# Preparing f64 weights in small VectorE steps, transposing k on TensorE, and fixed places for staged weights, in attention followed by two MLPs

## The chip, the cores and the metric

The kernel runs on one core of one Trainium2 chip. The metric is the device time of one execution in microseconds (us), lower is better. The engines are named as the profile names them: PE (TensorE, matmuls), PEld (its weight loads), DVE (VectorE), ACT (ScalarE), POOL (GpSimd) and SP (SyncE, which here only issues DMAs). Each engine works through its own instructions in order; a DMA issue is an instruction of the engine that issues it.

## The reference

Linear attention over 8 batches and 8 heads, then two MLPs on the 4608 tokens, one after the other. All arithmetic is f32; the weights arrive as f64.

```python
q_s = softmax(q, axis=-1)             # over head_dim 64, q is (8, 8, 576, 64)
k_s = softmax(k, axis=2)              # over the 576 positions
kv = np.einsum('bhsd,bhse->bhde', k_s, v)
x = np.einsum('bhsd,bhde->bhse', q_s, kv)
x = x.transpose(0, 2, 1, 3).reshape(4608, 512)
h = x @ w_in1;  x = (h * sigmoid(h)) @ w_out1              # (512, 2048), (2048, 512)
h = x @ w_in2;  out = (h * clip(h + 3, 0, 6) / 6) @ w_out2
```

## The kernel before

**Cycles.** The work on PE is a list of 144 cycles, g = 0 to 143. A cycle takes one block of 512 tokens and one pair p (0 to 7) of 128-column tiles of w_in with the matching rows of w_out; nine token blocks make one MLP, so cycles 0 to 71 are the first MLP and 72 to 143 the second. Cycles 0 to 7 (`first_cycle`, the first token block) use plain f32 matmuls. From cycle 8 on, `cycle` uses Strassen's scheme on split operands: seven `product`s of 128x256 matmuls into the PSUM banks A, B and C, each of three matmuls (high and low parts), and eight pieces `G` of the output product of the cycle before, into y. Bank A's left half is copied to B by ACT (L653), DVE adds s = B + s5 (L664), A + s (L669) and B + s5 (L674); then `bend` applies the activation (ACT L515 or L517, DVE L519) and splits the result into gs. PE can start its next product into B only when DVE has read B at L664. Bank D serves the attention. `side(k)`, k = 0 to 7, is called between the pieces of a cycle; there the attention and the weight preparation are woven in, and the order of these calls is the order of the instructions on each engine.

**Attention.** A unit u is a batch and two heads, 32 units. The four units of batch 0 run ahead of the cycles, those of batch 1 within cycles 0 to 7, the others later; `events` maps a tick (8 g + k) to the calls. In batch 1 the exponent of k in its natural layout is made by sending the row maximum through DRAM (`at_sendnm`, L304: nmd<-nm; `at_shift`, L310: nb<-nmd, both issued on ACT), a subtraction on POOL (`at_sub`, L315) and an exp on ACT (`at_exp`, L319).

**Weights.** A pair is staged as 1 MB of f64 words (st<-w_dram, `feed`, L90, on SP) and turned into f32 by `converting`: Abs on ACT into a tile "size" (L99), then four DVE instructions (L101, L102, L107, L112). For w_in, `operands_w` makes four sums s (L155) and splits both into the 1.8 MB operand "ring" (or r), high part on ACT, low part on DVE; `keep_w` stores it to DRAM (wd, on SP), and `load_w` brings it back two cycles ahead of its use (ring<-wd). For w_out, `split_out` makes woh (ACT) and wol (DVE). The first MLP's weights are prepared in cycles 0 to 14; the second's from cycle 56 on. There "size" shares one buffer ("ok") with the sums s. Staging has two buffers in both places. These functions are generators: each `yield` ends a step, and `pump(k)` takes k steps, whatever they cost:

```python
            if late and g > LATE:
                pump({NC - 2: (1, 0, 0, 0, 1, 1, 0, 0), NC - 1: (1, 0, 0, 0, 0, 1, 0, 0)}.get(p, (2, 0, 0, 0, 1, 1, 2, 0))[k])
```

Of the kernel before, what the change touches and what calls it, by code (L numbers as in the profile page):

```python
# [8 lines left out]
F32 = mybir.dt.float32  # L9
# [8 lines left out]
P = 128  # L18
# [17 lines left out]
def attention_two_mlps(ctx: ExitStack, tc: tile.TileContext, kqT, kv5, qn, w1, w2, out):  # L36
# [26 lines left out]
    def bank(name):  # L63
        if "D" in banks:
            return banks["D"]
        return banks["pool"].tile([P, 512], F32, tag="b", name=name)
# [14 lines left out]
    fed = [0]  # L81

    def feed(k=1):
        for m, p, i in stream[:k]:
            if m == 0:
                t = z_p.tile([P, 2 * DM, 2], U32, tag=f"z{fed[0] % 2}", name="st")
            else:
                t = m2_p[0].tile([P, 2 * DM, 2], U32, tag="st", name="st", bufs=2)
            fed[0] += 1
            nc.sync.dma_start(out=t.rearrange("p n w -> p (n w)"), in_=(w1, w2)[m][i, p])  # L90
            staged[m, p, i] = t
        del stream[:k]

    def converting(w, m, p, i):
        t = staged.pop((m, p, i))
        low, high = t[:, :, 0], t[:, :, 1]
        bits = w.bitcast(U32)
        size = (z_p if m == 0 else m2_p[0]).tile([P, 2 * DM], F32, tag="z3" if m == 0 else "ok", name="size")
        nc.scalar.activation(out=size, in_=f32(high), func=AF.Abs)  # L99
        yield  # L100
        nc.vector.tensor_scalar_max(size, size, SMALLEST)  # L101
        nc.vector.tensor_scalar(  # L102
            out=bits, in0=size.bitcast(U32), scalar1=3, scalar2=0x3FFFFFF8,
            op0=ALU.logical_shift_left, op1=ALU.bitwise_and,
        )
        yield
        nc.vector.scalar_tensor_tensor(  # L107
            out=bits, in0=high, scalar=0xC0000000, in1=bits,
            op0=ALU.bitwise_and, op1=ALU.bitwise_or,
        )  # L110
        yield
        nc.vector.scalar_tensor_tensor(  # L112
            out=bits, in0=low, scalar=29, in1=bits,
            op0=ALU.logical_shift_right, op1=ALU.bitwise_or,
        )
        if m == 0:
            feed()

    active = []

    def pump(k):
        while active and k > 0:
            try:
                next(active[0])
            except StopIteration:
                active.pop(0)
            k -= 1
# [7 lines left out]
    def convert_in(p):  # L135
        raw_in[p] = w = w_pool[p].tile([P, 2 * DM], F32, tag=f"a{p}", name="wi")
        yield from converting(w, 0, p, 0)

    def convert_out(p):
        raw_out[p] = w = w_pool[p].tile([P, 2 * DM], F32, tag=f"b{p}", name="wo")  # L140
        yield from converting(w, 0, p, 1)
# [5 lines left out]
    def operands_w(r, w, s):  # L147

        a22, a11, a12, a21 = (w[:, j * 256:(j + 1) * 256] for j in range(4))
        s1, s2, s3, s4 = (s[:, j * 256:(j + 1) * 256] for j in range(4))  # L150
        for o, x, y, op in (
            (s1, a21, a22, ALU.add), (s2, s1, a11, ALU.subtract),
            (s3, a11, a21, ALU.subtract), (s4, a12, s2, ALU.subtract),
        ):
            nc.vector.tensor_tensor(out=o, in0=x, in1=y, op=op)  # L155
        yield
        w3, s4 = (t.rearrange("p (s n) -> p s n", n=256) for t in (w[:, :768], s))
        split(r[:, 0, :3], r[:, 1, :3], w3)
        yield
        split(r[:, 0, 3:], r[:, 1, 3:], s4)  # L160

    def keep_w(m, p, r):
        wd[m, p] = d = dram.tile([P, 14 * 256], F32, tag=f"wd{m}{p}", name="wd")
        nc.sync.dma_start(out=d, in_=f32(r).rearrange("p h s n -> p (h s n)"))

    def prepare_in(p):
        r = ring_tile(NC + p)
        s = z_p.tile([P, 2 * DM], F32, tag="z2", name="s")
        yield from operands_w(r, raw_in.pop(p), s)
        yield  # L170
        yield
        keep_w(0, p, r)

    def split_out(m, p, w):
        h = w_pool[p].tile([P, 2 * DM], F32R, tag=f"a{p}", name="woh")
        q = (p - 1) % 9
        l = w_pool[q].tile([P, 2 * DM], F32R, tag=f"b{q}", name="wol")
        split(h, l, w)
        wo[m, p] = h, l

    def second_in(p):
        w = m2_p[0].tile([P, 2 * DM], F32, tag="w", name="w")
        yield from converting(w, 1, p, 0)
        yield
        s = m2_p[0].tile([P, 2 * DM], F32, tag="ok", name="s")
        r = m2_p[0].tile([P, 2, 7, 2 * P], F32R, tag="r", name="r")
        feed()
        yield from operands_w(r, w, s)
        yield
        keep_w(1, p, r)  # L190

    def second_out(p):
        w = m2_p[0].tile([P, 2 * DM], F32, tag="w", name="w")
        yield from converting(w, 1, p, 1)
        yield
        feed()
        split_out(1, p, w)
# [145 lines left out]
    def at_trk(u):  # L343
        k, e = un[u]["k"], un[u]["e"]
        b0, b1 = bank("tk0"), bank("tk1")
        for j in range(4):
            nc.tensor.transpose(b0[:, j * P:(j + 1) * P], k[:, j * P:(j + 1) * P], ident)
# [528 lines left out]
```

## Time and profile before

| | |
|---|---|
| median of 3 runs (lowest, highest) | 1767.19 us (1765.88, 1771.6) |
| the profiled execution | 1764.48 us, its span 1762.4 us |
| PE busy | 1659.3 us (94%) |
| DVE busy | 1044.0 us (59%) |
| ACT busy | 739.9 us (42%) |
| POOL busy | 185.4 us (11%) |
| DMA | 400.59 MB, mean 227 GB/s |

The span counts from the first to the last instruction; 2.1 us of the execution lie around it. Busy shares are means over the whole span, and its stages differ: the rows further down take them apart by stage, with the first matmul into bank C as the mark of a cycle.

### The profile page before, as it was taken

To read this page: it belongs to the slowest core of one execution; us is meant where nothing else is said; L and a number is where in the kernel's file an instruction comes from. 1 tells how busy PE (TensorE), PEld (TensorE's weight loads), DVE (VectorE), ACT (ScalarE), POOL (GpSimd) and SP (SyncE) were. 2 spreads that over 40 slices of the span, in tenths; PEclk is the share of its full clock that TensorE was granted. 3 is DMA by queue.
4 is the path that set the end of the run, shared out by engine and by line. 5 is a ranking of instruction groups with operands and counts; after the bars stand their busy time and mean duration, and the time that the engine had idled before them with its cause. 6 is when DMAs were issued, how large, how long until landed. Compare 5 with 4: busy or idle time off the path is not lost.

```text
span 1762.4 us, 25043 instructions
## 1 busy us (share of the span) xinstructions
PE 1659.3 (94%) x9796; PEld 1423.1 (81%) x9796; DVE 1044.0 (59%) x1733; ACT 739.9 (42%) x1392; POOL 185.4 (11%) x128
## 2 busy tenths in 40 slices
PE   7788999999999999999998899999999999999994
PEld 4334887888888898897777789999999999999994
DVE  7888677465656657467877764545453535353531
ACT  5434555444544445444444433333343434343431
POOL 2221223222222122200000000000000000000000
PEclk9899999999999999999999999999999999999997
DMA  8789969999999999868886746564546555555540
GB/s 218 226 264 274 269 161 283 252 228 248 235 281 256 229 243 260 241 236 328 308 308 270 290 164 226 186 227 168 215 172 227 185 223 189 194 200 207 207 169 24
DMA packets 72189, 400.59 MB, mean 227 GB/s; under 512 B 20872, under 2 KB 24456, under 8 KB 46472
## 3 DMA queue, kind: packets, MB, share of 16 engines
q1 hardware_dynamic: 70920, 398.72, 71.8%
q8 instruction: 78, 1.28, 0.3%
q10 hardware_dynamic: 1152, 0.26, 0.1%
q14 instruction: 39, 0.32, 0.1%
HBM read 350.49 MB, written 48.47 MB: 226 GB/s over the span
## 4 chain that ended last, share of the span: by engine, by line
PE 67%; DMA 14%; DVE 11%; ACT 4%; issue 2%; SPq 1%; POOL 0%; ACTq 0%; DVEq 0%; POOLq 0%
PE y L73 11%; PE y L74 11%; PE y L75 11%; PE B L73 5%; PE B L75 5%; PE B L74 5%; PE A L73 4%; DMA ring<-wd 4%; PE A L74 4%; PE A L75 4%; DMA q<-qn_dram 3%; DMA nmd<-nm 2%; DMA st<-w_dram 2%; PE C L75 1%; PE C L73 1%
## 5 line engine op out<-in xcount | busy, mean ns | idle before, releaser
L70 DVE TENSOR_TENSOR gs<-g,gs 128x512 fp32r<-128x512 f32 x272 | 195.3, 718 | 151.7 <-ACT gs L69 150.6
L73 PE MATMUL B<-o,ring 128*128 128x256 f32 x816 | 234.7, 288 | 37.3 <-DVE s L664 24.2
L69 ACT CAST gs<-g 128x512 fp32r<-128x512 f32 x272 | 168.6, 620 | 206.5 <-DVE g L519 206.1
L73 PE MATMUL A<-op,ring 128*128 128x256 f32 x816 | 232.7, 285 | 12.6 <-DMA ring<-wd 10.4
L74 PE MATMUL A<-op,ring 128*128 128x256 f32 x816 | 232.1, 284 | 1.2 <-DVE op L70 1.1
L75 PE MATMUL A<-op,ring 128*128 128x256 f32 x816 | 231.7, 284 | 0.0
L75 PE MATMUL B<-o,ring 128*128 128x256 f32 x816 | 230.7, 283 | 0.0
L74 PE MATMUL B<-o,ring 128*128 128x256 f32 x816 | 230.4, 282 | 0.0
L73 PE MATMUL y<-woh,gs 128*128 128x512 f32 x576 | 227.8, 395 | 0.0
L74 PE MATMUL y<-wol,gs 128*128 128x512 f32 x576 | 227.8, 395 | 0.0
L75 PE MATMUL y<-woh,gs 128*128 128x512 f32 x576 | 224.5, 390 | 0.0
L73 PEld LDWEIGHTS B<-o,ring 128*128 128x128 f32 x816 | 154.9, 190 | 72.5 <-DVE s L664 36.7
L73 PE MATMUL y<-gs,woh 128*128 128x512 f32 x512 | 205.4, 401 | 0.0
L74 PE MATMUL y<-gs,woh 128*128 128x512 f32 x512 | 203.1, 397 | 0.0
L75 PE MATMUL y<-gs,wol 128*128 128x512 f32 x512 | 200.9, 392 | 0.0
L73 PEld LDWEIGHTS A<-op,ring 128*128 128x128 f32 x816 | 156.7, 192 | 22.7 <-ACT o L69 4.2
L74 PEld LDWEIGHTS B<-o,ring 128*128 128x128 f32 x816 | 154.8, 190 | 15.1 <-issue 0.5
L74 PEld LDWEIGHTS A<-op,ring 128*128 128x128 f32 x816 | 156.9, 192 | 7.5 <-DVE op L70 2.1
L75 PEld LDWEIGHTS A<-op,ring 128*128 128x128 f32 x816 | 157.0, 192 | 0.0
L75 PEld LDWEIGHTS B<-o,ring 128*128 128x128 f32 x816 | 154.6, 189 | 0.0
L517 ACT ACTIVATE g<-A,half 128x512 f32<-128x512 f32 x72 | 49.6, 688 | 247.8 <-DVE A L669 247.8
L664 DVE TENSOR_TENSOR s<-B,s 128x256 f32<-128x256 f32 x136 | 57.3, 421 | 152.0 <-PE B L75 150.0
(145 smaller groups left out, 2993.3 us busy)
## 6 DMA issues: line engine op xcount, KB each, us to landing
ring<-wd SPq DMA_DIRECT2D x134, 1792.0 KB, 7.9
st<-w_dram SPq DMA_DIRECT2D x32, 1024.0 KB, 9.0
ev<-kv_dram SPq DMA_DIRECT2D x28, 640.0 KB, 9.9
wd<-ring SPq DMA_DIRECT2D x8, 1792.0 KB, 13.8
wd<-r SPq DMA_DIRECT2D x8, 1792.0 KB, 10.5
kq<-kqT_dram SPq DMA_DIRECT2D x24, 576.0 KB, 8.1
q<-qn_dram SPq DMA_DIRECT2D x32, 288.0 KB, 8.8
yd<-y SPq DMA_DIRECT2D x9, 1024.0 KB, 12.2
```

Of the source, the lines that this page charges most:

```text
L69: nc.scalar.copy(hi, src)
L70: nc.vector.tensor_tensor(out=lo, in0=src, in1=f32(hi), op=ALU.subtract)
L73: nc.tensor.matmul(o, lhsT=wh, rhs=xh, start=start, stop=False, **kw)
L74: nc.tensor.matmul(o, lhsT=wh, rhs=xl, start=False, stop=False, **kw)
L75: nc.tensor.matmul(o, lhsT=wl, rhs=xh, start=False, stop=stop, **kw)
L517: nc.scalar.activation(out=a, in_=hb, func=AF.Relu, scale=1.0 / 6.0, bias=half)
L664: nc.vector.tensor_tensor(out=s2, in0=B_[:, lo], in1=s5, op=ALU.add)
```

## The change

Three things are changed together.

1. **Weight preparation is a list of steps with a cost each**, the DVE time in us that a step is reckoned at (0 for ACT's). `pump(more, keep)` gives a credit, at most 2.6 us with what was kept, and takes steps while the credit covers the next. In cycles 0 to 7 each side gives 1.75; in the late cycles (from 57 on) only sides 0 to 3 give any. `chain` puts a pair's Abs ahead of the last step of the pair before it. Abs writes straight into the weight tile, so "size" is gone; the second MLP's sums take the staging tile's memory, and its weight tile has two buffers. `keep` (the store of the operand) and the second MLP's `feed` are issued on ACT instead of SP. In cycles 8 to 15, `split_out`'s high part comes at side 0 and its low part at side 1; pairs 6 and 7 of w_in are prepared at fixed sides of cycles 12 to 15.
2. **k of batch 1 is transposed on TensorE** (`at_trk` through bank C, as batch 0 does already), instead of the way through DRAM, POOL and exp; its k chunks are no longer loaded.
3. **Staging of the first MLP has five places at the start and three afterwards** (z0, z1 and the tile of operands 3 and 5, and at the start the two ring buffers); five pairs are requested before cycle 0 instead of two. Operands 3 and 5 share one tile.

```diff
+    HOMES = ("z0", "z1", "op35", "ring", "ring")
 
     def feed(k=1):
         for m, p, i in stream[:k]:
...
+            elif 3 <= fed[0] < 5:
+                t = ring_p.tile([P, 2, 7, 2 * P], F32R, tag="ring", name="st").rearrange("p h s n -> p (h s n)")
...
+                home = HOMES[fed[0] if fed[0] < 3 else (fed[0] - 5) % 3]
...
+            e = nc.scalar if m else nc.sync
+            e.dma_start(out=t.rearrange("p n w -> p (n w)"), in_=(w1, w2)[m][i, p])
...
+    def pump(more, keep=False):
+        credit[0] = min(more + (credit[0] if keep else 0.0), 2.6)
+        while steps and steps[0][0] <= credit[0] + 0.01:
+            cost, fn = steps.pop(0)
+            credit[0] -= cost
+            fn()
...
+            nc.scalar.activation(out=w, in_=f32(t[:, :, 1]), func=AF.Abs)
...
+            if m == 0 and done[0] not in (3, 4):
+                feed()
+            done[0] += 1
+
+        return [(0, magnitude), (0.7, floor), (0.7, shift), (1.2, sign), (1.2, low)]
...
+        def keep():
+            wd[m, p] = d = dram.tile([P, 14 * 256], F32, tag=f"wd{m}{p}", name="wd")
+            nc.scalar.dma_start(out=d, in_=f32(x["r"]).rearrange("p h s n -> p (h s n)"))
+
+        return [
+            (0.85, lambda: sums(0)), (0.85, lambda: sums(1)), (0, lambda: high(0)), (0.95, lambda: low(0)),
+            (0.6, lambda: high(1)), (0.6, lambda: low(1)), (0.5, keep),
+        ]
...
             plan = [
-                (-19, at_soft), (-18, at_sendnm), (-17, at_kexp), (-16, at_qexp), (-15, at_shift), (-14, at_knorm),
-                (-13, at_norm), (-12, at_sub), (-9, at_exp), (-9, at_trq, 0), (-8, at_trq, 1),
+                (-18, at_soft), (-17, at_kexp), (-16, at_qexp), (-14, at_trk, 0), (-14, at_knorm), (-13, at_norm),
+                (-12, at_trk, 1), (-9, at_trq, 0), (-8, at_trq, 1),
             ]
...
-            if late and g > LATE:
-                pump({NC - 2: (1, 0, 0, 0, 1, 1, 0, 0), NC - 1: (1, 0, 0, 0, 0, 1, 0, 0)}.get(p, (2, 0, 0, 0, 1, 1, 2, 0))[k])
+            if late and g > LATE and k < 4:
+                pump({NC - 1: (1.2, 0.8, 0.8, 0), 0: (1.2, 1.2, 1.2, 0.7)}.get(p, (2.4, 1.2, 1.2, 0.7))[k], keep=k > 0)
...
-            pump(2 if k in (1, 2, 4, 6) else 1)
+            pump(FIRST, keep=True)
...
+        if g == 1:
+            steps.extend(words_in + convert_out(g) + pre)
+        else:
+            steps.extend(pre[:4] + words_in + pre[4:] + convert_out(g))
```

On ACT at the start of the cycles (first to third cycle), before. The rows are issues and work of the first unit of batch 1 (k, q, nm, ev), the Abs of staged weights (size<-st) and the cycles' activations (g).

```order
L99 ACTIVATE size<-st 128x1024
L515 ACTIVATE g<-A 128x512
L304 DMA nmd<-nm 128x1
L296 ACTIVATE k,ks<-k,nm 128x576
L99 ACTIVATE size<-st 128x1024
L515 ACTIVATE g<-B 128x512
L299 ACTIVATE q<-q 96x768
L310 DMA nb<-nmd 128x128
L99 ACTIVATE size<-st 128x1024
L515 ACTIVATE g<-A 128x512
L319 ACTIVATE ev<-ev 128x640
L372 COPY qf<-D 128x288
```

The same place now:

```order
L122 ACTIVATE wi<-st 128x1024
L587 ACTIVATE g<-A 128x512
L122 ACTIVATE wo<-st 128x1024
L587 ACTIVATE g<-B 128x512
L364 ACTIVATE k,ks<-k,nm 128x576
L367 ACTIVATE q<-q 96x768
L416 COPY ev<-C 128x512
L122 ACTIVATE wi<-st 128x1024
L587 ACTIVATE g<-A 128x512
```

The two DMA issues and the exp of ev are gone; a copy of the transposed k out of bank C stands in their place.

On DVE in the late cycles, at the change from the eighth to the ninth token block (cycles 63 and 64), before. w<-st and s<-w are weight preparation, op and o are the next block's operands, s<-B is the row that the next product into B waits for.

```order
L70 TENSOR_TENSOR gs<-g,gs 128x512
L107 SCALAR_TENSOR_TENSOR w<-st,w 128x1024
L70 TENSOR_TENSOR op_1045<-rest,op_1045 128x512
L70 TENSOR_TENSOR o_1018<-tx,o_1018 128x512
L70 TENSOR_TENSOR o_1019<-t_7669,o_1019 128x512
L112 SCALAR_TENSOR_TENSOR w<-st,w 128x1024
L155 TENSOR_TENSOR s<-w 128x256
L155 TENSOR_TENSOR s<-s,w 128x256
L155 TENSOR_TENSOR s<-w 128x256
L155 TENSOR_TENSOR s<-w,s 128x256
L664 TENSOR_TENSOR s_7817<-B,s_7794 128x256
L669 TENSOR_TENSOR A<-A,s_7817 128x256
```

The same place now:

```order
L70 TENSOR_TENSOR gs<-g,gs 128x512
L70 TENSOR_TENSOR op_1008<-rest,op_1008 128x512
L70 TENSOR_TENSOR o_1006<-tx,o_1006 128x512
L70 TENSOR_TENSOR o_1007<-t_7639,o_1007 128x512
L128 TENSOR_SCALAR w<-w 128x1024
L745 TENSOR_TENSOR s_7785<-B,s_7770 128x256
L134 SCALAR_TENSOR_TENSOR w<-st,w 128x1024
L750 TENSOR_TENSOR A<-A,s_7785 128x256
L140 SCALAR_TENSOR_TENSOR w<-st,w 128x1024
L755 TENSOR_TENSOR B<-B,s_7770 128x256
```

Ahead of s<-B stood six weight instructions; now one does, and the long ones stand behind it, one between each two of DVE's rows on the banks.

On ACT in cycle 65, now. r<-w and r<-st are the high parts of an operand, DMA wd its store, DMA st the next staging.

```order
L736 COPY B<-A 128x256
L739 COPY s_7869<-C 128x256
L197 CAST r<-w 128x768
L197 CAST r<-st 128x1024
L122 ACTIVATE w<-st 128x1024
L205 DMA wd<-r 128x3584
L587 ACTIVATE g<-A 128x512
L96 DMA st<-w_dram 128x2048
L69 CAST gs<-g 128x512
```

The two issues stood on SP before; now they stand between ACT's rows of the cycle. The next row of the cycle, g<-A, reads bank A after DVE's A + s.

## Rows read from the trace of the kernel before

**Rows 1.** Busy time by stage: us, PE, PEld, DVE, ACT, POOL, granted clock, DMA share, GB/s.

```profile
31.30:173.50 142.20, 122.81 (x331) 58.53 (x331) 119.07 (x155) 56.56 (x91) 29.70 (x17) 0.93 0.86 242
281.00:771.50 490.50, 476.47 (x2952) 422.08 (x2951) 295.67 (x535) 228.12 (x477) 116.53 (x76) 0.99 0.94 244
771.50:1059.20 287.70, 262.06 (x1587) 229.53 (x1586) 213.08 (x328) 128.06 (x212) 0.00 (x0) 0.99 0.74 282
```

**Rows 2.** Timeline of PE, first matmul into C of cycles 8, 16, 48, 56, 80, 143.

```profile
176.34 0.41 PE L73 MATMUL C<-op,ring 128*128 128x256 f32 x1
...
281.02 0.28 PE L73 MATMUL C<-op,ring 128*128 128x256 f32 x1
...
677.26 0.28 PE L73 MATMUL C<-op,ring 128*128 128x256 f32 x1
...
771.54 0.28 PE L73 MATMUL C<-op,ring 128*128 128x256 f32 x1
...
1059.20 0.28 PE L73 MATMUL C<-op,ring 128*128 128x256 f32 x1
...
1723.63 0.28 PE L73 MATMUL C<-op,ring 128*128 128x256 f32 x1
```

**Rows 3.** Waits, 31 to 173.5 us: who waited for whom, us, times, longest.

```profile
PE D L357 <- ACT qf L372: 8.6, 2, 8.1
PE D L357 <- issue: 7.3, 3, 3.7
...
ACT size L99 <- DMA st<-w_dram: 23.8, 7, 8.7
...
ACT size L99 <- DMA nmd<-nm: 7.1, 2, 5.8
```

**Rows 4.** Timeline, first unit of batch 1: ACT, POOL, PE.

```profile
35.09 0.34 ACTq L304 DMA_DIRECT2D nmd<-nm  x1
...
43.85 0.33 ACTq L310 DMA_DIRECT2D nb<-nmd  x1
...
51.82 1.89 POOL L315 TENSOR_TENSOR ev<-ev,nb 128x640 f32<-128x640 f32 x1 [6.49 <-DMA nb<-nmd]
...
54.82 0.74 PE L357 MATMUL D<-ident,q 96*128 96x96 f32 x3 [8.08 <-ACT qf L372]
```

**Rows 5.** Timeline: transposes of k in batch 0 on PE.

```profile
15.80 1.11 PE L347 MATMUL tk<-ident,k 128*128 128x128 f32 x4
16.71 0.42 PE L348 MATMUL tk<-ident,k 128*64 128x128 f32 x1
```

**Rows 6.** Timeline: POOL's subtraction, DVE's L102 beside it, and L102 alone.

```profile
73.92 1.54 POOL L315 TENSOR_TENSOR ev<-ev,nb 128x640 f32<-128x640 f32 x1 [4.04 <-DMA nb<-nmd]
...
74.06 1.94 DVE L102 TENSOR_SCALAR wo<-size 128x1024 uint32<-128x1024 uint32 x1
...
93.89 0.69 DVE L102 TENSOR_SCALAR wo<-size 128x1024 uint32<-128x1024 uint32 x1
```

**Rows 7.** Waits of PE, 173.5 to 281 us; then 771.5 to 1059.2 us.

```profile
PE B L73 <- DVE s L664: 5.9, 3, 2.6
...
PE B L73 <- DVE s L664: 13.2, 10, 2.3
PE B L73 <- ACT B L653: 12.3, 8, 2.4
```

**Rows 8.** Timeline, cycles 64 and 65: DVE, PE, ACT, PE.

```profile
865.80 1.22 DVE L112 SCALAR_TENSOR_TENSOR w<-st,w 128x1024 uint32<-128x1024 uint32 x1
...
868.52 0.42 DVE L664 TENSOR_TENSOR s<-B,s 128x256 f32<-128x256 f32 x1
...
869.00 0.38 PE L73 MATMUL B<-o,ring 128*128 128x256 f32 x1 [1.54 <-DVE s L664]
...
876.72 1.12 ACT L99 ACTIVATE size<-st 128x1024 f32<-128x1024 f32 x1 [1.29 <-DVE r L70]
...
878.66 0.39 PE L73 MATMUL B<-o,ring 128*128 128x256 f32 x1 [1.71 <-ACT B L653]
```

More of the change, by code (lines that the diff above doesn't have):

```diff
@@ L119, in attention_two_mlps @@
[L119 to L127, printed above, removed]
+    steps = []
+    credit = [0.0]
+    def pump(more, keep=False):
[4 more added lines that the diff above has]
+            fn()
+    done = [0]
@@ L181, in second_in, with operands_w, sums, parts @@
[L181 to L197, printed above, removed]
+    def operands_w(m, p, new_r, new_s, get_w):
+        x = {}
+        def sums(k):
+            w = get_w()
+            if k == 0:
+                x["s"] = new_s()
+            a22, a11, a12, a21 = (w[:, j * 256:(j + 1) * 256] for j in range(4))
+            s1, s2, s3, s4 = (x["s"][:, j * 256:(j + 1) * 256] for j in range(4))
+            for o, a, b, op in (
+                (s1, a21, a22, ALU.add), (s2, s1, a11, ALU.subtract),
+                (s3, a11, a21, ALU.subtract), (s4, a12, s2, ALU.subtract),
+            )[2 * k:2 * k + 2]:
+                nc.vector.tensor_tensor(out=o, in0=a, in1=b, op=op)
+        def parts(k):
+            src, n = ((get_w()[:, :768], 3), (x["s"], 4))[k]
+            o = slice(0, 3) if k == 0 else slice(3, 7)
+            return x["r"][:, 0, o], x["r"][:, 1, o], src.rearrange("p (s n) -> p s n", n=256)
+        def high(k):
+            if k == 0:
+                x["r"] = new_r()
+            h, l, src = parts(k)
+            nc.scalar.copy(h, src)
+        def low(k):
+            h, l, src = parts(k)
+            nc.vector.tensor_tensor(out=l, in0=src, in1=f32(h), op=ALU.subtract)
+        def keep():
[5 more added lines that the diff above has]
+        ]
@@ new lines, in prepare_in, with split_out, high, low @@
+    def prepare_in(p):
+        return operands_w(
+            0, p, lambda: ring_tile(NC + p), lambda: z_p.tile([P, 2 * DM], F32, tag="z2", name="s"), lambda: raw_in[p]
+        )
+    def split_out(m, p, get_w):
+        def high():
+            wo[m, p] = (
+                w_pool[p].tile([P, 2 * DM], F32R, tag=f"a{p}", name="woh"),
+                w_pool[(p - 1) % 9].tile([P, 2 * DM], F32R, tag=f"b{(p - 1) % 9}", name="wol"),
+            )
+            nc.scalar.copy(wo[m, p][0], get_w())
+        def low():
+            h, l = wo[m, p]
+            nc.vector.tensor_tensor(out=l, in0=get_w(), in1=f32(h), op=ALU.subtract)
+        return [(0, high), (1.2, low)]
@@ L199, in load_w, with chain @@
+    def chain(jobs, second_mlp=False):
+        out = []
+        for k, j in enumerate(jobs):
+            if k and len(jobs[k - 1]) < 10:
+                out += j[:1]
+                j = j[1:]
+            elif k:
+                out[-1:-1] = j[:1]
+                j = j[1:]
+            if k and second_mlp and len(jobs[k - 1]) >= 10:
+                j = j[:1] + [(0, feed)] + j[1:]
+            out += j
+        return out
     def load_w(g):
@@ L797, in attention_two_mlps @@
             at_norm(3, nc.vector)
-            pump(1)
+            for _, fn in step[:3]:
+                fn()
             turn(1)
```

208 lines of the change are left out of this document (106 added, 102 removed).

## The prediction

> **What bounds the kernel now.** I began with PE's pace by cycle, read from the first matmul into bank C [rows 2]. From cycle 80 to 143 there are 63 cycles in 664.4 us, 10.55 us each: this is what a cycle costs when nothing disturbs it. Three stretches are slower. Cycles 56 to 80, where the second MLP's weights are prepared, take 287.7 us where 24 undisturbed cycles would take 253.1: 34.5 us too long. Cycles 8 to 16 take 104.7 us; cycles 48 to 56, which carry as much attention work, take 94.3: 10.4 us too long. And before cycle 8 lies the stage of plain matmuls, 142.2 us with PE busy for 122.8, so 19.4 us idle [rows 1]. These sums, about 64 us, are all that the change can reach; the rest is the same instructions before and after.
>
> Next, what PE waits for. In the first stage it is bank D, evacuated late by ACT [rows 3], and the reason is ACT's order: the row maximum of the first unit leaves at 35.09, ACT can issue its return only at 43.85, POOL subtracts at 51.82, and PE, which needs work queued behind this on ACT, starts again at 54.82 after 8.1 us [rows 4]. ACT also stands 23.8 us at the Abs of weights that have not landed, and 7.1 us behind such a returning maximum [rows 3]. In the late stage PE waits 13.2 us for DVE's s and 12.3 us for ACT's copy of A to B [rows 7]. The two have different causes. At cycle 64 DVE runs a long weight instruction at 865.80 and then the four sums before it comes to s at 868.52, and PE has lost 1.5 us. At cycle 65 ACT waits 1.3 us at an Abs, because "size" lies in the buffer from which DVE has yet to split s (r); the copy to B is queued behind it, and PE loses 1.7 us [rows 8].
>
> **First stage, cycles 0 to 7.** Removed: four round trips through DRAM with ACT held at them, four POOL subtractions, and most of the waiting for weights, as five pairs are requested before cycle 0 and three places serve afterwards. Added on PE: five transposes for each of four units; in batch 0 four took 0.91 us to the start of the fifth, which took 0.42 [rows 5], so 1.3 x 4 = 5.3 us. ACT's copies take the place of its exp over as many columns: nothing, since ACT is busy for 56.6 of 142.2 us [rows 1]; without that cover they would cost under 1 us a unit. On DVE a subtraction that runs beside it costs: L102 took 1.94 us next to one and 0.69 alone [rows 6], so up to 4 x 1.25 = 5.0 us come back. The operand's store now stands on ACT and must wait for DVE's low part; the next Abs is queued behind it, and DVE's next weight step behind that. This is between nothing and a whole Abs, 1.1 us [rows 8], for six stores; I take 0.5 each, as one of DVE's other rows usually lies between: 3 us. DVE then needs 119.1 - 5 + 3 = 117 us [rows 1] and PE 122.8 + 5.3 = 128.1. PE is the bound, and if 3 of its 19.4 us of idling stay, the stage gains 19.4 - 5.3 - 3 = 11 us. Lower bound 3: waits of 11 us stay, because DVE at 117 of 131 us has little slack. Upper bound 20: no wait stays (14), and the granted clock, 0.93 in the mean here against 0.99 later [rows 1], comes back for most of a further 7% of PE's time.
>
> **Cycles 8 to 15.** DVE's wol goes behind s, and the operands of pairs 6 and 7 come in single sums and splits. PE's waits for s are 5.9 us here [rows 7]. At the block's end (cycles 15 and 16) the next operands, not the weights, crowd DVE, so not all of the 10.4 us goes. I take 5, with bounds of 1 (the split of both halves still stands before s at side 0) and 9.
>
> **Late stage, cycles 56 to 79.** "size" no longer exists and the weight tile has two buffers, so the Abs waits for no split of the sums: the 12.3 us behind ACT's copy have no cause left. For s, the order shows at cycle 64 one short instruction (0.7 us by L102 alone [rows 6]) where L112 and four sums took 2.7 us [rows 8] and L107 stood ahead of them; PE lost 1.5 us there, so that wait goes. In other cycles the credit allows 2.4 us ahead of s, and nothing at sides 4 to 7, where up to four steps stood. Of the 34.5 us, the 25.5 of listed waits and the 9 that PE takes to restart, I leave 0.2 us for each of 21 cycles, as DVE's long steps now stand ahead of its rows on A and B, and 2 us for each of the three changes of block, where ten operand instructions of 0.6 to 0.7 us come on top: 10 us. Gain 24, bounds 10 and 34. DVE's total bounds nothing: 213.1 us [rows 1] fit in 263.
>
> The 32 issues moved to ACT (16 stores, 16 stagings) take ACT 0.33 us each at most, the length of such an issue [rows 4]; ACT is busy for 128.1 of 287.7 us in the late stage, so I cost the issues themselves at nothing. What matters is their wait: a rival, below. SP loses those waits, so its ring loads are issued no later than before. Cycles 16 to 55 and 80 to 143, and operands 3 and 5 in one tile (written at sides 3 and 5 of a block's last cycle, after the products that read them), count as nothing, plus or minus 3 us.
>
> **The sum.** 11 + 5 + 24 = 40 us from the profiled execution's 1764.5 us gives 1724.5. That execution lies 2.7 us under the median of the runs, so I predict 1727 us. The bounds together are 14 and 63 us.
>
> **The rivals.** *VectorE still decides in the late stage* (0.17). DVE has 8.9 of every 10.55 us to do (213.1 over 24 cycles), and a step of 1.2 us that misses its gap may delay B + s5 or g as it delayed s. Then only ACT's 12.3 us go: 40 - 12 = 28 us gain, 1739 us. For it speaks DVE's load; against it that the undelayed rows A + s and B + s5 have PE's two products and two output pieces as slack.
>
> *The transfers hold the first stage* (0.10). The DMA engines are busy for 0.86 of it at 242 GB/s [rows 1], 34.4 MB; the k chunks of batch 1 save only 1.3 MB. At a full share that rate becomes 281 GB/s and 118 us, below PE's 128; at the 245 GB/s or so that a core gets with small packets about it would be 135 us or more. Staging would stay late and the stage gain 0 to 3 us: 1737 us. The Trainium skill, "DMA: Bandwidth & Descriptors", section "Issuing engines are not separate DMA queues", says that issuing from another engine gives no more bandwidth; no run here shows two heavy queues yet, and by that rule the move to ACT brings these bytes no sooner.
>
> *ACT is held at its DMA issues, and the kernel gets slower* (0.05). Each of the 32 issues can wait in ACT's order for DVE's low part or the freed staging tile, and the copy to B is queued behind. Before, a held ACT cost PE 12.3 / 8 = 1.5 us a time [rows 7]. At 32 x 1.5 = 49 us against a gain of 40 it would end at 1736 + 40 = 1776 us. It decides from 40 / 32 = 1.25 us an issue on. Against it: in the order the row behind a store, g<-A, itself waits for DVE's A + s, which stands behind that low part on DVE, so ACT would stand there anyway. The same page's section "Anatomy of one DMA — SWDGE (gpsimd) path" says that the wait for a semaphore is served on the issuing engine's sequencer before dispatch. By that rule ACT does stand at each issue; ACT's 43.85 issue, and the 7.1 us of Abs queued behind such issues, agree.
>
> *No difference that can be measured* (0.04): the stalls move within the cycles as the work on DVE is the same, and the transposes eat the rest; 1764 to 1770 us.
>
> **How the numbers follow.** My forecast has 0.64: 1727 us, its own range 1708 to 1745. The two smaller gains (0.27) lie at 1737 to 1739, inside it or just at its edge. The range of 1708 to 1751 reaches to the lower bounds (14 us) and leaves out the slower case, no change, and the last of the upper bound. A measurement of this kernel tells 0.3%, 5 us, from no change. Faster: 0.64 + 0.17 + 0.10 = 0.91; same 0.04; slower 0.05.
>
> **What the profile of the changed kernel would show.** The first matmul into C near 165 us instead of 176; cycles 8 to 16 in about 100 us; cycles 56 to 80 in about 264 us; no wait of PE for ACT's copy to B, few for s; no nmd<-nm before cycle 5, and ACT's waits for st<-w_dram in the first stage down from 23.8 us to a few. It would prove me wrong if ACT showed long waits at its wd<- and st<- issues, if PE waited for DVE's B + s5 or the splits instead of s, or if the Abs still waited for st<-w_dram with the DMA share near 1.

## The result, and the profile after

The changed kernel takes 1744.88 us in the median of four runs (1743.33 to 1745.34), the kernel before 1766.54 us beside it: a ratio of 0.987, 95% interval 0.985 to 0.989. It is faster by 21.7 us; I had forecast 40. The profiled execution takes 1744.62 us with a span of 1742.8, so the spans differ by 19.6 us. These stand against the terms of the prediction as follows, each stage taken between first matmuls into C.

| stage | before | after | gain | forecast |
|---|---|---|---|---|
| up to cycle 8 | 176.34 | 166.39 | 9.95 | 11 |
| cycles 8 to 15 | 104.68 | 104.36 | 0.3 | 5 |
| cycles 16 to 55 | 490.52 | 497.52 | -7.0 | 0 |
| cycles 56 to 79 | 287.66 | 271.33 | 16.3 | 24 |
| cycles 80 to 142 | 664.43 | 664.44 | 0 | 0 |

The marks, first matmuls into C of cycles 8, 16, 56, 80 and 143, are shown with the timeline further down.

The forecast of 11 us was worked out for the stage of [rows 1], from the first plain matmul of cycle 0 to the first matmul of cycle 8. That stage ran from 31.27 to 173.48 us and now runs from 29.97 to 164.44: it gained 7.7 us. Of the other 2.2 of the table's 9.95, 1.3 lie ahead of cycle 0 and 0.9 in the first product of cycle 8.

The busy times of this stage and the next three (columns as in [rows 1]):

```profile
29.97:164.44 134.47, 122.61 (x350) 58.45 (x351) 116.58 (x158) 57.24 (x96) 26.20 (x13) 0.99 0.66 232
166.39:270.75 104.36, 98.16 (x586) 83.14 (x585) 77.47 (x125) 55.00 (x105) 29.60 (x16) 0.98 0.84 231
270.75:768.27 497.52, 476.89 (x2953) 420.73 (x2951) 298.92 (x540) 229.10 (x479) 116.21 (x75) 0.99 0.91 240
768.27:1039.60 271.33, 258.76 (x1586) 230.61 (x1585) 206.90 (x328) 127.69 (x212) 0.00 (x0) 0.98 0.77 299
```

In the first stage the DMA share is down from 0.86 to 0.66 and the granted clock up from 0.93 to 0.99. PE is busy for 122.6 us, about as long as before (122.8), although it now also makes the transposes.

What PE waits for, stage by stage (us in all, times, longest), answering to [rows 3, 7]:

```profile
PE D L426 <- POOL q L406: 5.1, 2, 2.7
PE D L426 <- ACT rest L496: 2.4, 3, 1.3
...
PE D L426 <- issue: 1.5, 2, 1.0
...
PE B L73 <- DVE B L755: 3.7, 2, 2.4
PE B L73 <- DVE s L745: 1.5, 3, 1.0
PE A L73 <- DMA ring<-wd: 1.0, 1, 1.0
...
PE B L73 <- DVE s L745: 11.3, 11, 1.9
PE A L73 <- DMA ring<-wd: 7.1, 6, 2.3
...
PE B L73 <- DVE s L745: 7.2, 3, 5.7
PE B L73 <- DVE B L755: 4.8, 2, 4.0
```

The first three lines are the first stage, the next three cycles 8 to 15, then two of the middle, and the last two the late stage. In the late stage PE's waits for ACT's copy to B (12.3 us before) are gone, but single waits of 5.7 and 4.0 us have come. They belong to two cycles: 66 takes 16.35 us and 75 takes 18.46, where nearly all others take 10.55. Together these two lose 13.7 us. The timeline shows how: first PE's five marks, which answer to [rows 2], then, in time order engine by engine, ACT, SP, DVE and PE at the first place, and ACT and PE at the second.

```profile
166.39 0.28 PE L73 MATMUL C<-op,ring 128*128 128x256 f32 x1
...
270.75 0.28 PE L73 MATMUL C<-op,ring 128*128 128x256 f32 x1
...
768.27 0.28 PE L73 MATMUL C<-op,ring 128*128 128x256 f32 x1
...
1039.60 0.28 PE L73 MATMUL C<-op,ring 128*128 128x256 f32 x1
...
1704.04 0.28 PE L73 MATMUL C<-op,ring 128*128 128x256 f32 x1
...
869.12 0.33 ACTq L205 DMA_DIRECT2D wd<-r  x1
...
869.53 0.45 ACTq L96 DMA_DIRECT2D st<-w_dram  x1
...
883.99 1.12 ACT L122 ACTIVATE w<-st 128x1024 f32<-128x1024 f32 x1 [5.33 <-DMA st<-w_dram]
...
872.48 0.32 SPq L267 DMA_DIRECT2D ring<-wd  x1
872.84 1.23 SPq L519 DMA_DIRECT2D xr<-yd  x1
...
885.14 0.69 DVE L125 TENSOR_SCALAR w<-w 128x1024 f32<-128x1024 f32 x1 [4.88 <-ACT w L122]
885.75 0.43 DVE L755 TENSOR_TENSOR B<-B,s 128x256 f32<-128x256 f32 x1
...
886.23 0.39 PE L73 MATMUL B<-o,ring 128*128 128x256 f32 x1 [3.95 <-DVE B L755]
...
971.07 0.45 ACTq L96 DMA_DIRECT2D st<-w_dram  x1
...
986.20 1.12 ACT L122 ACTIVATE w<-st 128x1024 f32<-128x1024 f32 x1 [6.31 <-DMA st<-w_dram]
...
988.43 0.58 PE L73 MATMUL B<-o,ring 128*128 128x256 f32 x1 [5.66 <-DVE s L745]
```

Read it from the end. PE waits for DVE's B + s5; DVE had stood 4.9 us at L125, a weight step ahead of that row; L125 waited for ACT's Abs; the Abs had stood 5.3 us for staged words. They were requested 14.5 us earlier, right behind a 1.8 MB store on the same queue, and SP sent a ring load and the 1 MB xr load 3 us after them. DVE and ACT do not cause this: the staged words are late.

### The profile page after: what moved, and what is told of

Read it like the earlier page. It is cut to its first block, busy times and chain, and to the rows that moved or that the text cites. A ratio compares the mean times of both kernels' runs of the same rounds, so it can differ in the third digit from the quotient of the medians.

```text
span 1742.8 us, 25018 instructions
## 1 busy us (share of the span) xinstructions
PE 1655.8 (95%) x9816; PEld 1422.0 (82%) x9816; DVE 1034.8 (59%) x1733; ACT 739.3 (42%) x1396; POOL 182.6 (10%) x124
## 4 chain that ended last, share of the span: by engine, by line
PE 70%; DMA 15%; DVE 9%; ACT 2%; issue 1%; POOL 1%; SPq 1%; ACTq 0%; POOLq 0%; DVEq 0%
PE y L73 12%; PE y L74 11%; PE y L75 11%; PE B L73 5%; PE B L74 5%; PE B L75 5%; PE A L73 4%; PE A L74 4%; PE A L75 4%; DMA ring<-wd 4%; DMA qr<-qr 4%; DMA st<-w_dram 3%; DMA q<-qn_dram 2%; PE C L75 2%; PE C L74 2%; PE C L73 2%
## 5 line engine op out<-in xcount | busy, mean ns | idle before, releaser
L70 DVE TENSOR_TENSOR gs<-g,gs 128x512 fp32r<-128x512 f32 x272 | 202.0, 743 | 157.9 <-ACT gs L69 156.4
L73 PE MATMUL A<-op,ring 128*128 128x256 f32 x816 | 231.5, 284 | 10.5 <-DMA ring<-wd 8.6
```

The lines of the kernel that those rows point to most:

```text
L70: nc.vector.tensor_tensor(out=lo, in0=src, in1=f32(hi), op=ALU.subtract)
L73: nc.tensor.matmul(o, lhsT=wh, rhs=xh, start=start, stop=False, **kw)
```

## The experiments

Three theories were open. **A:** the words are requested too late, since the second MLP's sums now lie in the staging place and hold it until the operand is split. **B:** the transfers are too slow whatever the order. **C:** ACT's queue serves these words worse than SP's did. Beside that: whether the cause named in the prediction for ACT's late copy to B was right, which part made the first stage's gain, and why the middle lost 7 us.

The experiments were made on three chips, B to D; A stands for the chip of the result, which is not on record and may be one of them. The chip matters: the kernel before took 1766.5 us on A, 1769.0 on B, 1788.8 on C, 1788.9 and 1790.1 on D. Ratios are to the kernel before on the same chip; the stages (us) come from one profiled execution each.

| run | chip | ratio (95% interval) | first C of 8 | 8 to 16 | 16 to 56 | 56 to 80 |
|---|---|---|---|---|---|---|
| before | A | 1 | 176.3 | 104.7 | 490.5 | 287.7 |
| changed | A | 0.987 (0.985 to 0.989) | 166.4 | 104.4 | 497.5 | 271.3 |
| e1_third_place | B | 0.982 (0.979 to 0.986) | 171.0 | 104.1 | 499.1 | 257.7 |
| e2_stsp | B | 0.984 (0.981 to 0.986) | 165.9 | 105.1 | 498.2 | 261.0 |
| e3_size_alone | B | 1.000 (0.998 to 1.002) | 174.1 | 106.0 | 494.1 | 284.8 |
| e4_k_dram | B | 0.993 (0.991 to 0.995) | 185.2 | 105.1 | 491.5 | 266.2 |
| e5_two_places | C | 0.985 (0.982 to 0.988) | 171.9 | 104.1 | 513.5 | 270.0 |
| e6_keep_sp | C | 0.976 (0.974 to 0.979) | 166.5 | 105.4 | 509.7 | 260.7 |
| e7_later_sides | C | 0.983 (0.980 to 0.987) | 168.9 | 105.5 | 512.7 | 268.3 |
| e8_third_sp | C | 0.979 (0.975 to 0.982) | 165.8 | 107.2 | 516.4 | 261.5 |
| e9_idle_trips | D | 0.985 (0.981 to 0.989) | 172.8 | 107.6 | 507.6 | 268.2 |
| e10_transposes_alone | D | 0.997 (0.994 to 0.999) | 171.5 | 107.4 | 507.8 | 287.5 |
| e11_changed_again | D | 0.988 (0.983 to 0.993) | 169.9 | 103.7 | 511.5 | 271.9 |
| e12_third_keep_sp | D | 0.975 (0.972 to 0.978) | 167.2 | 106.1 | 513.3 | 257.7 |

Cycles 80 to 143 take 664.43 or 664.44 us in every one of them. Other columns scatter where the code is the same. The first stage is that of the changed kernel in six rows (changed, e1, e2, e7, e8, e11), and cycle 8 starts at 165.8 to 171.0 us in them; on chip B alone e1 and e2 lie 5 us apart. With the old first stage it starts at 176.3 (before) and 174.1 us (e3). So 3 us in that column decide nothing. In the late stage the changed kernel's code takes 268.2 to 271.9 us in five rows.

**A third staging place.** From cycle 56 on z1 (8 KB) holds only the 4 KB of operand 4, and z2 is free:

```diff
-                t = m2_p[0].tile([P, 2 * DM, 2], U32, tag="st", name="st", bufs=2)
+                if late_fed[0] % 3 < 2:
+                    t = m2_p[0].tile([P, 2 * DM, 2], U32, tag="st", name="st", bufs=2)
+                else:
+                    t = z_p.tile([P, 2 * DM, 2], U32, tag="z1", name="st")
+                late_fed[0] += 1
...
+        if i == 4 and n == B - 1:
+            op_x[4] = z_p.tile([P, 2, 2, HT], F32R, tag="z2", name="o4")
...
-            feed(2)
+            feed(3)
```

> The changed kernel with a third staging place in the second MLP (operand 4 moves to the free 4 KB of z2 at cycle 55, its old place z1 takes staged words) and three pairs requested at cycle 56. Theory A, the two long Abs waits (5.3 and 6.3 us) come from a request made too late, because a place is held by the sums until the operand is split: no wait of ACT for st over 1 us, PE without the 5.7 and 4.0 us waits for s and B, cycles 56 to 80 in 257 to 260 us instead of 271.3, the kernel at 1731 to 1734 us. Theory B, the transfers themselves are too slow there (a ring load, the xr load and staging at once): as many bytes in the same stretch, so ACT still stands at st for 8 us or more, cycles 56 to 80 at 269 to 272 us, the kernel at 1743 to 1746 us.

Cycles 56 to 80 took 257.7 us, 13.6 less than in the changed kernel and 4.6 from undisturbed. ACT's list of waits there has none for staged words any more, and PE's waits in that stretch are these:

```profile
PE A L73 <- DMA ring<-wd: 1.1, 3, 0.6
PE B L73 <- DVE s L752: 1.0, 1, 1.0
PE B L73 <- DVE B L762: 0.9, 1, 0.9
```

Theory A holds and B falls: the same bytes pass in less time (314 GB/s against 299). The kernel as a whole gained less than that, 0.982 (on B) beside the changed one's 0.987 (on A), since its cycle 8 started at 171.0 us.

**Staging on SP, at the same place in the program.**

```diff
-            e = nc.scalar if m else nc.sync
+            e = nc.sync
```

> The changed kernel with the second MLP's staging issued on SP again, at the same place in the program; the operand's store stays on ACT. Theory A (request too late by the place held): the request can't come earlier, so the two waits stay at 4 to 8 us each and cycles 56 to 80 at 269 to 274 us, 1743 to 1748 us. Theory C, the ACT queue serves these words more slowly (landing in 10.6 us in the median against 9.0 us on SP before): both waits shrink by 1.6 us or more each, cycles 56 to 80 at 264 to 268 us, 1738 to 1742 us. If SP, held at these issues, sends ring loads late instead, PE shows waits for ring of over 3 us in all in cycles 56 to 80.

261.0 us, below the range that I gave for theory C. So the time of the request is not all of it: with the request at the same place the words land sooner from SP. The timeline of this run at the first of the two places:

```profile
869.98 0.33 SPq L96 DMA_DIRECT2D st<-w_dram  x1
...
873.71 1.07 SPq L519 DMA_DIRECT2D xr<-yd  x1
...
881.72 1.12 ACT L122 ACTIVATE w<-st 128x1024 f32<-128x1024 f32 x1 [2.20 <-DMA st<-w_dram]
```

11.7 us from issue to Abs instead of 14.5. Of the landings that the traces tell, the median of the late stage's staged words is 9.2 us against 10.9, and that of the store, now alone on ACT's queue, 11.0 against 7.6 (two and three of eight stores): what the words gain the store seems to lose. The Trainium skill, "DMA: Bandwidth & Descriptors", section "Queues, rings and completion order", says that each DMA engine takes turns, packet by packet, between the queues that have work. By that rule store and staging in one queue share one turn while SP's loads have the other; these landings agree.

**The store on SP, staging on ACT.**

```diff
-            nc.scalar.dma_start(out=d, in_=f32(x["r"]).rearrange("p h s n -> p (h s n)"))
+            nc.sync.dma_start(out=d, in_=f32(x["r"]).rearrange("p h s n -> p (h s n)"))
```

> The changed kernel with the operand's store on SP again in both MLPs; the second MLP's staging stays on ACT. In the first stage ACT's 15.7 us at the Abs behind the store (which waits for DVE's low part) should vanish; my term of 3 us for it says cycle 8 starts 2 to 4 us earlier, at 162 to 165 us; rival, ACT has room there and PE waits for others: 165.5 to 168 us. In cycles 56 to 80, if staged words come late because the 1.8 MB store stands ahead of them in ACT's queue: the two long waits at st fall under 2.5 us each, 258 to 263 us. If it is the number of bytes under way (store, ring, xr and staging, whichever queue): the waits stay at 4 to 7 us, 268 to 273 us. In all 1732 to 1740 us by the first reading of both, 1742 to 1747 by the second.

Late stage: 260.7 us; ACT's waits for staged words shrink to 5.2 us in three, the longest 2.5. With two places it is enough that store and staging do not both stand in ACT's queue; which of them is on SP makes no difference. (In the kernel before both stood in SP's queue, and ACT did not wait for staged words in the late stage, but that stage was 16 us longer.) In the first stage ACT stood for 15.7 us at the Abs behind the store, which waits for DVE's low part; this row of the changed kernel is gone here:

```profile
ACT wo L122 <- DVE ring L201: 15.7, 5, 5.3
```

Cycle 8 starts at 166.5 us, no sooner than in the other runs on that chip with all staging places (165.8 and 168.9). So ACT had room for these waits.

**Third place and staging on SP.**

> The third staging place and the second MLP's staging on SP together. The third place alone left cycles 56 to 80 at 257.7 us, SP alone at 261.0; 24 undisturbed cycles are 253.1. If either cure removes the same stalls, the two together give 256 to 259 us and the kernel 1729 to 1737 us, by how the first stage and the middle fall; if SP, held at three places' issues, sends ring loads late, PE waits for ring over 3 us and the stretch takes 261 to 266 us.

261.5 us: no better than either alone. The two cures are for one stall, and the second reading holds: PE's waits for s and B + s5 are down to 1.0 and 0.9 us, but it now waits for ring loads, which stand behind staging in SP's order (the longest was issued at 991.22 us, right behind two staging requests at 985.67 and 990.78):

```profile
PE A L73 <- DMA ring<-wd: 3.5, 3, 2.5
```

**The kernel before with a buffer of its own for "size".**

```diff
-        size = (z_p if m == 0 else m2_p[0]).tile([P, 2 * DM], F32, tag="z3" if m == 0 else "ok", name="size")
+        size = z_p.tile([P, 2 * DM], F32, tag="z3" if m == 0 else "z2", name="size")
```

> The kernel before with one edit: in the second MLP, size gets a buffer of its own (z2) and no longer shares the sums' buffer. The prediction's reading (the 12.3 us that PE waits for ACT's copy to B come from the Abs ahead of it, which waits for the buffer): these waits vanish, cycles 56 to 80 take 274 to 277 us instead of 287.7, the kernel 1753 to 1757 us. Rival: DVE's long steps ahead of s decide anyway, the time moves into waits for s (13.2 us before, then 20 or more), and the kernel gains under 4 us: 1763 to 1767 us.

The ratio is 1.000, the stretch 284.8 us. The waits for ACT's copy stay, which neither reading had foreseen (PE, late stage):

```profile
PE B L73 <- ACT B L653: 12.0, 10, 2.4
PE B L73 <- DVE s L664: 10.9, 7, 2.3
```

In the kernel before, the Abs stands for its buffer in one of the eight cases alone, the one of [rows 8]; in the other seven the row that waits ahead of the copy is a high-part copy (woh or r) that waits for DVE, in two of them with an Abs between that waits for nothing. ACT and DVE at the longest case in this run:

```profile
1004.38 1.04 ACT L69 CAST woh<-w 128x1024 fp32r<-128x1024 f32 x1 [3.70 <-DVE w L112]
1005.33 0.37 ACT L653 COPY B<-A 128x256 f32<-128x256 f32 x1
...
999.93 0.69 DVE L101 TENSOR_SCALAR size<-size 128x1024 f32<-128x1024 f32 x1
...
1003.12 1.23 DVE L112 SCALAR_TENSOR_TENSOR w<-st,w 128x1024 uint32<-128x1024 uint32 x1
```

ACT's copy of the weight's high part waits for the last of DVE's four conversion steps, which the old list puts at the end of one cycle, and the copy to B is queued behind it. In the changed kernel ACT waits for the same step nearly as long, eight times again, and it costs PE nothing, since no copy to B stands next behind it. ACT's row before and now:

```profile
ACT woh L69 <- DVE w L112: 19.0, 8, 3.7
ACT woh L223 <- DVE w L140: 17.6, 8, 2.6
```

**k through DRAM again, the rest as changed** (the old plan, its transfers on ACT, the full ev load).

```diff
-                (-18, at_soft), (-17, at_kexp), (-16, at_qexp), (-14, at_trk, 0), (-14, at_knorm), (-13, at_norm),
-                (-12, at_trk, 1), (-9, at_trq, 0), (-8, at_trq, 1),
+                (-19, at_soft), (-18, at_sendnm), (-17, at_kexp), (-16, at_qexp), (-15, at_shift), (-14, at_knorm),
+                (-13, at_norm), (-12, at_sub), (-9, at_exp), (-9, at_trq, 0), (-8, at_trq, 1),
```

> The changed kernel with batch 1's k made as before (row maximum through DRAM, POOL's subtraction, ACT's exp; k chunks loaded), all else as changed. If the way through DRAM was the larger part of the first stage's loss (8.1 us at bank D, 7.1 us of ACT at the returning maximum), cycle 8 starts at 172 to 177 us instead of 166.4 and the kernel takes 1750 to 1756 us. Rival, the staging places and the steps made the gain: cycle 8 starts at 161 to 168 us (PE saves 5.3 us of transposes), the kernel takes 1739 to 1747 us.

Cycle 8 starts at 185.2 us, later than in the kernel before and above both ranges. The first stage's row, and PE's and ACT's waits in it:

```profile
31.30:185.18 153.88, 128.84 (x338) 59.98 (x337) 125.12 (x163) 59.49 (x97) 34.51 (x17) 0.92 0.73 219
```

```profile
PE D L424 <- POOL q L404: 15.4, 3, 6.1
PE D L424 <- issue: 4.1, 1, 4.1
...
ACT ev L384 <- POOL ev L380: 10.9, 4, 4.8
ACT wi L122 <- DMA nmd<-nm: 7.2, 2, 4.9
ACT ring L197 <- DMA nmd<-nm: 6.7, 2, 5.8
```

The weight steps had moved ahead and now stand behind the returning maximum on ACT. The granted clock is 0.92 again and PE busy for 128.8 us with fewer instructions than at 0.99.

**The transposes alone in the kernel before** (part 2 only: the transposes, the v chunks alone, the new ticks).

> The kernel before with part 2 alone: batch 1's k transposed on PE, its k chunks not loaded, units ten ticks apart; weight preparation and staging as before. The changed kernel without part 2 lost all of the first stage's gain (cycle 8 at 185.2 instead of 166.4). If the transposes are the whole gain of that stage, cycle 8 starts at 164 to 169 us here too. If they only pay together with the other two parts (ACT still stands at st, 23.8 us before), cycle 8 starts at 171 to 176 us. Cycles 56 to 80 stay at 284 to 289 us; cycle 36 takes 13 us or more and cycle 39 under 14.5, if these go with the transfers that are left out.

Cycle 8 at 171.5 us, in the range that I gave for transposes that pay only with the other parts; but it lies within 1.6 of the changed kernel on that chip (169.9), and ACT stands at st for only 9.2 us. From the first matmul of cycle 0, which starts late here (33.76 us), the stage takes 137.8 us, in the changed kernel on D 139.1. So the transposes alone bring about what all three parts bring there, as far as single executions tell; and parts 1 and 3 without them lose: 185.2 against 174.1 us (e3, with the old first stage) on chip B. As a whole this kernel is 5.8 us faster than the kernel before, from 1788.9 to 1783.1 us. The late stage is as before, 287.5 us, so its gain is not part 2's.

**Two staging places in the first MLP, operands 3 and 5 apart** (part 3 undone).

> The changed kernel with the first MLP's staging in two places (z0, z1) as before, two pairs requested before cycle 0, operands 3 and 5 in tiles of their own. Theory: with k transposed, PE and the attention chain bound the first stage, and the words arrive early enough from two places: cycle 8 starts at 165 to 169 us, the kernel at 1741 to 1747 us. Rival, the early requests carried part of the gain: ACT stands at st for 8 us or more in the first stage (none in the changed kernel, 23.8 before), cycle 8 starts at 171 to 177 us, the kernel at 1748 to 1756 us. For the middle (cycles 16 to 56; 490 to 494 us in the three runs with k through DRAM, 497.5 to 499.1 in the three with the transposes): if the shared tile of operands 3 and 5 costs the 7 us, 490 to 494 here; if it is the transposition's, 497 to 500; if it is only the scatter of single executions, anything in 490 to 500.

Cycle 8 at 171.9 us; ACT stands at st for 10.7 us, 10.0 of it at once:

```profile
ACT wo L118 <- DMA st<-w_dram: 10.7, 2, 10.0
```

The rival's wait is there and cycle 8 lies in its range, but its price is not shown: beside the other runs on chip C (165.8 to 168.9) it is 3 to 6 us, no more than the same code scatters by on chip B. The kernel's ratio, 0.985, is no worse than the changed kernel's 0.987 and 0.988. The late stage keeps its gain (270.0 us); with e10 this leaves part 1 for it. The middle, 513.5 us, lies among them (509.7 to 516.4), so the shared tile of operands 3 and 5 is not what makes it long.

**Later sides for pairs 6 and 7.**

```diff
-                for i in {0: (3, 5), 1: (6,)}.get(k, ()):
+                for i in {2: (3,), 3: (5, 6)}.get(k, ()):
...
-                if early and k in (2, 3, 5, 6):
-                    pre[-1][{2: 0, 3: 1, 5: 2, 6: 4}[k]][1]()
+                if early and k in (4, 5, 6):
+                    for i in {4: (0, 1), 5: (2,), 6: (4,)}[k]:
+                        pre[-1][i][1]()
```

> The changed kernel with another order in cycles 12 to 14 alone: the low parts of the operand of pairs 6 and 7 at sides 2 and 3 instead of both at side 0 (ahead of s), the sums at side 4 instead of 2 and 3. Theory, DVE's row of weight steps ahead of s and B + s5 makes cycle 13 16.1 us long (waits of 1.05 and 2.42 us): cycle 13 falls to 12.5 to 14 us, cycles 8 to 16 to 100 to 102.5 us instead of 104.4, the kernel to 1740 to 1743 us. Rival, the attention's chain at that place (kq, qm, ql late by transfers) sets it: cycles 8 to 16 stay at 103.5 to 106 us, the kernel at 1743 to 1747 us.

Cycle 13 fell from 16.1 to 12.7 us as expected, but cycle 14 rose from 11.8 to 13.9, and cycles 8 to 16 took 105.5. Of the crowding, 3.4 us moved and 2.1 came back one cycle later; cycles 10 and 12 are 1.1 and 1.3 us longer. The edit doesn't touch cycle 10; in cycle 12 it moves the sums, but this cycle takes 12.7 us in e8 too, without the edit. Inconclusive for the stage.

**The eight small transfers back, read by nobody.** In the runs so far cycle 36 takes 13.3 us or more without these transfers and 11.3 with them, and cycle 39 is shorter without them, though all engines have the same rows there.

```diff
-                (-18, at_soft), (-17, at_kexp), (-16, at_qexp), (-14, at_trk, 0), (-14, at_knorm), (-13, at_norm),
-                (-12, at_trk, 1), (-9, at_trq, 0), (-8, at_trq, 1),
+                (-18, at_soft), (-18, at_sendnm), (-17, at_kexp), (-16, at_qexp), (-14, at_trk, 0), (-14, at_knorm), (-13, at_norm),
+                (-12, at_trk, 1), (-9, at_trq, 0), (-9, at_shift), (-8, at_trq, 1),
```

> The changed kernel plus batch 1's eight small transfers alone: the row maximum to DRAM and back, issued on ACT as before, and read by nobody (k is transposed all the same). In all seven runs with the transposes cycle 36 took 13.3 to 18.0 us and cycle 39 13.0 to 14.2; in all three with k through DRAM 11.3 and 16.2 to 16.9, though every engine has the same instructions there in the same order. Theory: the middle depends on the sequence of transfers issued before it, so with the eight back, cycle 36 takes 11.3 to 12 us, cycle 39 16 to 17, and cycles 16 to 56 take 5 to 8 us less than in the changed kernel on the same chip. Rival: it depends on the time at which the cycles run or on the k chunks' loads, and cycle 36 stays at 13 us or more, cycle 39 under 14.5. The first stage: cycle 8 within 3 us of the changed kernel's, since nothing waits for these transfers.

> The changed kernel as it is, on the chip of the two runs above, as their measure: cycle 8 at 165 to 171 us, cycles 56 to 80 at 268 to 272, cycle 36 at 13 us or more; cycles 16 to 56 at 497 to 500 us on a chip like the first, 510 to 516 on one like that of the last four.

Cycle 36 takes 12.0 us and cycle 39 18.3 here; in the changed kernel on the same chip 16.4 and 14.1. The middle is 4.0 us shorter (507.6 to 511.5), a little less than I gave, but not by these two cycles: together they take 30.3 us here and 30.5 in the changed kernel. So the eight transfers move time from one cycle to the other. The place is one transfer, the spread of a unit's 1/sum of q (qr), for which POOL's multiplication waits. SP and POOL in the changed kernel on chip D, cycle 36:

```profile
527.33 1.09 SPq L326 DMA_DIRECT2D qr<-qr  x2
...
538.72 1.40 POOL L338 TENSOR_TENSOR kq<-kq,qr 128x576 f32<-128x576 f32 x1 [11.14 <-DMA qr<-qr]
```

The same in the run with the eight transfers, cycle 36 and then cycle 39:

```profile
532.24 1.53 SPq L326 DMA_DIRECT2D qr<-qr  x2
...
581.28 1.09 SPq L326 DMA_DIRECT2D qr<-qr  x2
...
538.13 1.43 POOL L338 TENSOR_TENSOR kq<-kq,qr 128x576 f32<-128x576 f32 x1 [5.38 <-DMA qr<-qr]
...
591.81 1.62 POOL L338 TENSOR_TENSOR kq<-kq,qr 128x576 f32<-128x576 f32 x1 [10.98 <-DMA qr<-qr]
```

From issue to multiplication cycle 36 has 11.4 us in one and 5.9 in the other; with the eight transfers it is cycle 39's that takes 10.5. In all fourteen executions the two kinds are apart: one of cycle 36's two spreads lands after 9.8 to 12.5 us in the ten without the eight transfers and both within 5.5 in the four with them, and cycle 39's after 5.5 to 6.7 and 9.1 to 10.4. ACT's copy of qh, DVE's ql and then s are behind POOL, and PE waits for s.

**Third place, and the store on SP.**

> The third staging place of the second MLP together with the operand's store on SP; staging stays on ACT. Alone they left cycles 56 to 80 at 257.7 and 260.7 us; 24 undisturbed cycles are 253.1. If the two take away the same waits and nothing new comes, 255.5 to 258 us, and the kernel at 0.975 to 0.982 of the kernel before (the changed kernel: 0.987 and 0.988). If three places let staging run ahead into the ring loads on SP, as with staging on SP at three places (261.5 us), PE waits for ring or for s again and the stretch takes 260 us or more.

257.7 us in the late stage, as with the third place alone, and 0.975 (0.972 to 0.978) in all: 1747.5 us beside 1790.1. With e6_keep_sp (0.976) it is the best version of the study. The changed kernel's own intervals, 0.985 to 0.989 and 0.983 to 0.993, lie above it. On chip D it is 18.0 us shorter than the changed kernel (1747.5 and 1765.5), and 14.2 of these are the staged words' in the late stage.

## Why the prediction was right and wrong

**First stage: the size near, partly by luck, and the way wrong.** 7.7 us for 11 over the stage that I forecast, in one pair of executions. I had PE at 128.1 us and 3 us of idling. It was busy for 122.6 and idle for 11.9. The transposes took PE 3.6 us where I had 5.3 (L415 2.5, L418 1.1), and the granted clock rose from 0.93 to 0.99, which I had only put into the upper bound, while of the waits at bank D some stayed (5.1, 2.4 and 1.5 us). Two errors, of 5.5 and 8.9 us, cancelled in part. That the round trips were to blame holds: without part 2 the gain turns into a loss. That DVE would need 117 us was right (116.6). The store's price at DVE, 3 us, was 4.1 by its waits for wo's Abs; ACT stood for 15.7 us behind its stores, one of my signs of being wrong, but moving the store away brought no time that can be told from the scatter. The rival of the transfers falls: the DMA share is 0.66.

**Cycles 8 to 15: wrong.** The step that failed is that DVE's wol behind s frees 5 of the 5.9 us that PE waited for s. Cycles 8 to 15 gained 0.3. The waits changed their names: B + s5 3.7, s 1.5, ring 1.0, together 6.2; waits for B + s5 I had named as a sign against me. The low parts and sums of pairs 6 and 7 now stand ahead of DVE's bank rows in cycle 13.

**Late stage: right for s, wrong for ACT's copy, blind for the staging.** I left 10 us over the undisturbed cycles; with the staged words in time (e1) 4.6 are left. So part 1 with words in time is worth 30 us, near my upper bound of 34, and the rival that VectorE decides falls: PE waits 1.0 us for s there. The 9 us that I counted as PE's restarting went with the waits: PE is busy for 254.8 us there, 262.0 before. But I gave the 12.3 us behind ACT's copy to the Abs waiting for the shared buffer, from one case [rows 8]; with that buffer separate 12.0 of them stayed. The cause was ACT's high-part copy standing at DVE's crowded steps ahead of the copy to B. It went with the new order of the steps, in which ACT still waits for DVE but the copy to B does not stand next behind. That a separate "size" alone is not enough is shown (e3); that the order alone is enough is not, as no run has the new order with "size" in the shared buffer. And 13.7 us were lost to late staged words. I weighed the 32 issues on ACT by what ACT loses at them, and found nothing; the loss was at the landing. A place that is held by the sums until the split, and a request behind a 1.8 MB store on its own queue, leave 14.5 us for words that need them all when a ring load and the xr load run too. I had named an Abs that still waits for st, with the DMA share near 1, as a sign against me; it came in the late stage, at a share of 0.77.

**Middle: counted as nothing, lost 7.0 us, cause open.** The eight transfers that part 2 removes set which of two cycles is long: with them or idle copies of them cycle 36 is 11.3 to 12.0 us, without 13.3 to 18.0; cycle 39 goes the other way (16.2 to 18.3, and 13.0 to 14.1). But the two together took 28.1 us before and 28.2 in the changed kernel, so nothing of the 7.0 us is in them; it is spread over many cycles. On one chip the middle is 491.5 and 494.1 with the transfers, 498.2 and 499.1 without (B), and 507.6 against 511.5 (D, e9 and e11). But on D the kernel before with the transposes alone lacks them too and has 507.8, so single executions scatter by as much. What makes one spread's landing depend on transfers of some hundred us earlier stays open too.

**The sum.** 11 + 5 + 24 became 9.95 + 0.3 + 16.3, less 7.0, which makes the 19.6 us between the spans. The time lies in the range because the lower bounds of the stages together were 14 us; the middle lies outside the 3 us that I gave it. Two slips in the sums changed nothing: the slower rival's 1776 us is 1727 + 49, and the range's upper end, counted from the median as the forecast was, would be 1753.

## What to carry to other kernels

Before a DMA issue is moved to another engine or its buffer put to a second use, work out when its words are needed, what frees the place, and what else is in its queue and on the way at that time; a wait at the consumer is then priced, not only the issue. A wait that occurs eight times is explained by the instruction ahead of it in most of the eight, not in the one that was looked at. And stage times of different kernels are compared on one chip, and more than one execution of it, before a few us in the middle are explained.

## What was not expected of the hardware

**Chips differ most where the DMA share is highest.** The changed kernel takes 1744.9 us on chip A and 1765.5 on D. In its profiled executions cycles 16 to 56, with a DMA share of 0.91 and 0.92, take 497.5 and 511.5 us, while cycles 56 to 80, at 0.77, differ by 0.6 and cycles 80 to 143 agree to 0.01 us.

**The landing of a small transfer depends on small transfers long before it.** The qr spread above lands about 5 or about 10 us after its issue, by place and not by chance: the slow one is in cycle 36 in all ten executions without the eight early transfers and in cycle 39 in all four with them, whatever the chip (A to D, and A, B and D). The Trainium skill, "DMA: Bandwidth & Descriptors", section "Queues, rings and completion order", says that a transfer's semaphore lands only after every earlier write of that DMA engine, across its queues. No run here shows the order within one DMA engine, so that is a lead and not a cause.

**PE's clock fell at single waits, and their sum does not tell where.** In the first stage the granted clock is 0.92 to 0.94 in the three runs that make k by way of DRAM (before, e3, e4) and 0.97 to 0.99 in all others. Idle time in all does not part them: PE is idle for 17.0 us at 0.94 (e3) and for 17.1 at 0.98 (e9). In the kernel before the clock is at the lower of its two levels, 1.2 GHz (0.50 of 2.4), from 48.9 to 59.1 and from 103.5 to 110.3 us, and both times PE stood in a wait when it fell, of 8.1 and of 3.7 us. In the changed kernel it is there once, from 74.7 to 78.1 us, from a wait of 2.4 us on. Yet a wait of 3.0 us in the kernel before, up to 131.9 us, has no fall. What it costs: at 0.92 PE was busy for 128.8 us with 338 instructions (e4), and the changed kernel's 350, at 0.99, took 122.6.
